# A decode layer on one core: 32 rows of wq by one indirect load of GpSimd instead of 512 columns by two side loads

## The chip, the cores and the metric

The kernel runs on one core of a Trainium2 chip. The metric is the device time of one execution in microseconds (us); the kernel before takes 137.85 us, the median of three runs (137.82 to 137.93). Engines are named as the profile names them: PE (TensorE), DVE (VectorE), ACT (ScalarE), POOL (GpSimd) and SP (SyncE, which issues most of the loads). PEld is PE's weight load, SPq and ACTq are the sequencers that issue DMAs.

## What is computed

One decode step of a transformer layer for a batch of 4 tokens with D = 1024, in bf16:

```
h  = x + attention(layernorm(x))          # 32 query heads, 4 kv heads, head size 128
h2 = h + (silu(hn @ w1) * (hn @ w3)) @ w2 # hn = layernorm(h), F = 3584
```

Attention projects the normed x with wq (1024 x 4096), takes the last W = 2048 positions of the K and V caches, scales by 128^-0.5, applies softmax, multiplies by V and projects with wo (4096 x 1024). Weights and cache together are some 55.6 million bytes, and each byte is used once.

## The kernel before

All weights and caches pass through one buffer, `ring`: 128 partitions by 81,920 columns of bf16 (`RING`, line 80). `plan` (line 129) lists the loads in their order, each with the column of the ring where it starts; `load_next` (line 149) issues the next entry. Nearly all are issued on SP's queue. The places, in columns:

- wq, rows 0 to 3 of each partition: 0 to 16,383; rows 4 to 7: 16,384 to 32,767. The view `wq_v` puts rows 8p to 8p + 7 of wq in partition p, so "row i" of a partition is row 8p + i of wq, with 4096 columns.
- K of the four batches: 32,768 to 65,535, four loads of 2 MB (`load_kv`).
- V of batch 0: 65,536 to 73,727, V of batch 1: 73,728 to 81,919. V of batches 2 and 3 go to 0 to 16,383, once the first half of wq is used.
- wo to 16,384 to 49,151, after the second half of wq and K of batches 0 and 1; w1 to 49,152 to 77,823, after K of batches 2 and 3 and V of batches 0 and 1; w3 to 0 to 28,671; w2 in four pieces.

A load into columns that are in use waits for the matmuls that read them. The tile framework adds these waits, and a wait where one of eight DMA semaphores is used again; it also settles each engine's order of instructions. Each engine runs its own in that order.

The work in order: x is loaded on ACT's queue, normed on DVE (lines 178 to 190), transposed on PE into `xnT` (line 194). q is computed by 512-column matmuls with `xnT[:, kc, :]` as weights (line 263), for the eight rows kc of each partition and the eight pieces of 512 columns, four of which fill different partitions of `q_ps`. q is scaled (lines 281, 282), transposed (line 285) and spread into `qz` (line 286). K is transposed in groups of eight tiles into one of four PSUM tiles (line 319), which DVE and ACT copy by turns to a `kT` tile (lines 323, 325; four buffers); each `kT` tile of two groups gives four scores matmuls (line 304). Then come softmax (lines 335 to 343), P's transposes (lines 350 to 360), P times V (line 382), wo (line 411), the second norm (lines 423 to 451), w1 and w3 (line 459) and w2 (line 492).

The part that the change replaces concerns row 7, the last of each partition, and of it the last 512 of 4096 columns. The main load of rows 4 to 7 (`load_tail`, line 123) stops 512 columns short. The 128 pieces of 512 columns come by two small loads (`load_side`, line 115), 20 partitions with four pieces each and 12 partitions with four pieces each, into two `kT` buffers. The matching values of the normed x are picked by two copies on DVE (line 206), transposed by eight small matmuls (line 211), copied from PSUM (line 218), and eight matmuls (line 273) with them as weights add the missing products to the last 512 columns of q, after row 3.

Of the kernel before, what the change touches and what calls it, by code (L numbers as in the profile page):

```python
# [10 lines left out]
P = 128  # L11
ACT = mybir.ActivationFunctionType
ALU = mybir.AluOpType
AX = mybir.AxisListType
BF16 = mybir.dt.bfloat16
FP32 = mybir.dt.float32


@with_exitstack
def kernel(  # L20
# [13 lines left out]
    nc = tc.nc  # L34

    B, _, D = A_x.shape
# [5 lines left out]
    KC = D // P  # L42
# [15 lines left out]
    ktpool = ctx.enter_context(tc.tile_pool(name="ktpool", bufs=4))  # L58
    wide = ctx.enter_context(tc.tile_pool(name="wide", bufs=2))
    const = ctx.enter_context(tc.tile_pool(name="const", bufs=1))  # L60
    act = ctx.enter_context(tc.tile_pool(name="act", bufs=1))
# [3 lines left out]
    JG = 4  # L65
    QD = P // JG
    RS = QD // B
    CQ = Hq * Dh // JG
# [11 lines left out]
    RING = 5 * 16384  # L80
# [8 lines left out]
    ring = stream.tile([P, RING], BF16)  # L89
# [19 lines left out]
    N_Q, N_F = Hq * Dh, F  # L109


    CE = 512
    SETS = [(0, 5, 4), (80, 3, 4)]

    def load_side(r0, ne, ns):

        t = ktpool.tile([P, JG * QD * 16], BF16, tag="kT")
        rows = A_wq[r0 * KC : (r0 + ne * 4 * ns) * KC, N_Q - CE : N_Q]
        rows = rows.rearrange("(t i k) n -> k i t n", i=ne, k=KC)[KC - 1]
        nc.sync.dma_start(out=t[: ne * 4, : ns * CE], in_=rows)  # L120
        return [t[: ne * 4, k * CE : (k + 1) * CE] for k in range(ns)]

    def load_tail(at, src, n, r0, m):

        t = ring[:, at : at + m * n]
        nc.sync.dma_start(out=t[:, : m * n - CE], in_=src[:, r0 * n : (r0 + m) * n - CE])
        return [t[:, k * n : (k + 1) * n] for k in range(m)]
    KIB = 512
    plan = [
        ("wq", load_rows, (0, wq_v, N_Q, 0, 4)),  # L130
        ("side", load_side, SETS[0]),
        ("side", load_side, SETS[1]),
        ("wq", load_tail, (32 * KIB, wq_v, N_Q, 4, 4)),
        ("k", load_kv, (64 * KIB, A_k_cache, 0)),
        ("k", load_kv, (96 * KIB, A_k_cache, 2)),
# [10 lines left out]
    loaded = {}  # L146
    cursor = [0]

    def load_next(n=1):
        for _ in range(n):  # L150
            if cursor[0] < len(plan):
                kind, f, args = plan[cursor[0]]
                loaded.setdefault(kind, []).extend(f(*args))
                cursor[0] += 1

    x_sb = act.tile([B, D], BF16)
    for c in range(2):
        nc.scalar.dma_start(out=x_sb[:, c * 512 : (c + 1) * 512], in_=x_flat[:, c * 512 : (c + 1) * 512])
    load_next(7)

    ident = const.tile([P, P], BF16)
    make_identity(nc, ident[:])
    eps_t = const.tile([P, 1], FP32)
    nc.vector.memset(eps_t[:], eps)

# [2 lines left out]
    for c in range(2):  # L168
        nc.sync.dma_start(
            out=x_q[c * 2 * QD : (c + 1) * 2 * QD : RS, :],  # L170
            in_=x_flat.rearrange("b (j c) -> j b c", j=JG)[2 * c : 2 * c + 2],
        )

    psA_cm = tc.tile_pool(name="psA", bufs=1, space=bass.MemoryType.PSUM)
    psA = psA_cm.__enter__()


    stats = act.tile([B, 2, nc.vector.BN_STATS_DIM], FP32)
    for c in range(2):
        nc.vector.bn_stats(out=stats[:, c, :], in_=x_sb[:, c * 512 : (c + 1) * 512])  # L180
    mv = act.tile([B, nc.vector.BN_AGGR_DIM], FP32)
    nc.vector.bn_aggr(out=mv[:], in_=stats[:])
    rstd = act.tile([B, 1], FP32)
    nc.scalar.activation(out=rstd[:], in_=mv[:, 1:2], func=ACT.Sqrt, bias=eps_t[:B], scale=1.0)
    nc.vector.reciprocal(out=rstd[:], in_=rstd[:])
    xn = act.tile([B, D], BF16)
    nc.vector.tensor_scalar(  # L187
        out=xn[:], in0=x_sb[:], scalar1=mv[:, 0:1], scalar2=rstd[:, 0:1],
        op0=ALU.subtract, op1=ALU.mult,
# [5 lines left out]
    xnT = act.tile([P, KC, B], BF16)  # L195
    nc.vector.tensor_copy(out=xnT[:], in_=tp_ps[:])


    NS = sum(ns for _, _, ns in SETS)
    ts_ps = psA.tile([P, NS, B], BF16, tag="kt1")  # L200
    xs = wide.tile([B, NS, 20], BF16, tag="w4k")
    sl = []
    for r0, ne, ns in SETS:
        v = xn[:, r0 * KC : (r0 + ne * 4 * ns) * KC]
        v = v.rearrange("b (s l i k) -> b k l i s", s=4, l=ns, i=ne)
        nc.vector.tensor_copy(
            out=xs[:, len(sl) : len(sl) + ns, : ne * 4].rearrange("b l (i s) -> b l i s", s=4),
            in_=v[:, KC - 1, :, :, :],
        )
        for l in range(ns):  # L210
            nc.tensor.transpose(
                out=ts_ps[: ne * 4, len(sl), :], in_=xs[:, len(sl), : ne * 4], identity=ident[:B, :B]
            )
            sl.append(ne * 4)
    xsT = act.tile([20, NS, B], BF16)
    k0 = 0
    for _, ne, ns in SETS:
        nc.vector.tensor_copy(out=xsT[: ne * 4, k0 : k0 + ns, :], in_=ts_ps[: ne * 4, k0 : k0 + ns, :])
        k0 += ns


    q_ps = psA.tile([P, CQ], FP32, tag="scores")
    nc.vector.memset(q_ps[:], 0.0)

    qz = act.tile([P, B, Hkv * QD + REP], BF16)
    nc.vector.memset(qz[:], 0.0)
    ident_f = const.tile([P, P], FP32)
    nc.vector.tensor_copy(out=ident_f[:], in_=ident[:])
# [3 lines left out]
        out=perm[:].rearrange("p (h dq) -> p h dq", dq=JG),  # L232
        in_=ident[:].rearrange("p (dq h) -> p h dq", dq=JG),
# [12 lines left out]
    for j in range(2, JG):  # L246
        nc.vector.tensor_tensor(
            out=same[:, 0, :], in0=same[:, 0, :], in1=ident[:, j * QD : (j + 1) * QD], op=ALU.add
# [3 lines left out]
        nc.vector.tensor_copy(out=same[:, j, :], in_=same[:, 0, :])  # L252


    for kc in range(KC):
        wq_t = loaded["wq"][kc]
        for hf in range(CQ // 512):
            for g in range(JG):
                c0 = g * CQ + hf * 512
                n = min(512, N_Q - CE - c0) if kc == KC - 1 else 512  # L260
                if n <= 0:
                    continue
                nc.tensor.matmul(  # L263
                    q_ps[QD * g : QD * g + B, hf * 512 : hf * 512 + n],
                    lhsT=xnT[:, kc, :],
                    rhs=wq_t[:, c0 : c0 + n],
                    start=(kc == 0),
                    stop=(kc == KC - 1 or (kc == KC - 2 and c0 + 512 == N_Q)),
                )
        if kc == RQ - 1:  # L270
            load_next()
            for k, np_ in enumerate(sl):
                nc.tensor.matmul(
                    q_ps[QD * (JG - 1) : QD * (JG - 1) + B, CQ - CE : CQ],
                    lhsT=xsT[:np_, k, :],
                    rhs=loaded["side"][k],
                    start=False,
                    stop=False,
                )
    q_sb = act.tile([P, CQ], BF16)  # L280
    nc.vector.tensor_single_scalar(out=q_sb[:, :512], in_=q_ps[:, :512], scalar=qscale, op=ALU.mult)
    nc.scalar.mul(out=q_sb[:, 512:], in_=q_ps[:, 512:], mul=qscale)
# [1 line left out]
    for r in range(REP):  # L284
        nc.tensor.transpose(out=qt_ps[:, r, :], in_=q_sb[:, r * Dh : (r + 1) * Dh], identity=ident[:])
    nc.vector.tensor_copy(
        out=qz[:, :, : Hkv * QD].rearrange("p b (g z) -> p b g z", g=Hkv)[:, :, :, :REP],
        in_=qt_ps[:].rearrange("p r (g x) -> p x g r", g=Hkv)[:, :B, :, :],
# [24 lines left out]
    for u, (b, n) in enumerate(units):  # L313
        k_v = loaded["k"][b]
        kT = ktpool.tile([P, NJ, P], BF16, tag="kT")
        for t in range(NJ // TB):
            kt_ps = psA.tile([P, TB, P], BF16, tag=f"kt{nt % 4}")
            for jj in range(TB):
                nc.tensor.transpose(  # L319
                    out=kt_ps[:, jj, :], in_=k_v[:, n * NJ + t * TB + jj, :], identity=ident[:]  # L320
# [21 lines left out]
        out=Pm[:], in_=scores_ps[:], func=ACT.Exp, bias=nmax[:], scale=1.0, accum_out=rsum[:]  # L342
# [6 lines left out]
    for c in range(NSB):  # L349
# [4 lines left out]
        for g in range(Hkv):  # L354
            if g % 2 == 0:
                nc.vector.tensor_scalar(  # L356
                    out=z[:, :, g, :], in0=pt_ps[:], scalar1=mask[:, g : g + 1], scalar2=None, op0=ALU.mult
# [10 lines left out]
        out=Dm[:], in0=ident[:].rearrange("p (g b r) -> p b g r", g=Hkv, b=B),  # L368
        scalar1=rinv[:, 0:1], scalar2=None, op0=ALU.mult,
# [10 lines left out]
    for b in range(B):  # L380
        for j in range(JK):
            nc.tensor.matmul(  # L382
                OT_ps[:, b, :],
                lhsT=loaded["v"][b][:, j, :],
                rhs=PTz[j // NJ][:, (j % NJ) * B + b, :, :],
                start=(j == 0),
                stop=(j == JK - 1),
# [21 lines left out]
    for i in range(IO):  # L409
        for j in range(JG):  # L410
            nc.tensor.matmul(  # L411
                y_ps[QD * j : QD * (j + 1), :],
                lhsT=o4[:, i, :, :].rearrange("p b s -> p (b s)"),
                rhs=loaded["wo"][i][:, j * CG : (j + 1) * CG],
                start=(i == 0),
                stop=(i == IO - 1),
# [27 lines left out]
        out=hn[:], in0=h1[:], scalar1=tot[:, 0:1], scalar2=rstd2[:, 0:1],  # L444
        op0=ALU.subtract, op1=ALU.mult,
# [4 lines left out]
        out=hnT[:].rearrange("p k x -> p (k x)"), in_=hn[:].rearrange("q (c k) -> q k c", k=KC)  # L450
# [3 lines left out]
    def gate_up(kind, out_ps):  # L454
# [27 lines left out]
        out=hgT[:].rearrange("p i x -> p (i x)"),  # L482
        in_=hg[:].rearrange("q s c -> q (s c)").rearrange("q (c i) -> q i c", i=IF),
# [18 lines left out]
    for i in range(R1, IF):  # L502
        for c, t in enumerate((ya_ps, yb_ps)):
            down(i, HC, c * HC, t, start=(i == R1), stop=(i == IF - 1), skip_group_check=True)
        if i == R2 - 1:
            for c, t in enumerate((ya_ps, yb_ps)):
                nc.tensor.matmul(
                    t[:, :HC], lhsT=ident_f[:], rhs=h2[:, c * HC : (c + 1) * HC],
                    start=False, stop=False, skip_group_check=True,
# [36 lines left out]
```

## Time and profile before

| what | value |
|---|---|
| time, median of three runs | 137.85 us |
| span of the profiled execution, first to last instruction | 136.0 us |
| PE busy | 72.3 us (53%) |
| DVE, ACT, POOL busy | 43.9, 31.0, 1.7 us |
| bytes read by DMA | 55.59 million, 409 GB/s over the span |
| share of the chain that ended last: DMA, PE, ACT, DVE | 54%, 25%, 11%, 5% |

The span leaves out what lies before the first and after the last instruction; the median is 1.85 us above it. The profile shows, for one execution, the busy share of each engine in 40 equal slices (3.4 us each), the chain of work that ended last followed back from the end, groups of equal instructions with their durations, and the DMA issues with the time to their landing. Times in it count from the first instruction. "x31" is a number of instructions, and what stands behind an arrow is what was waited for.

### The profile page before, as it was taken

What the parts mean: (1) busy time and instruction counts of PE and PEld (TensorE: products, weight loads), DVE (VectorE), ACT (ScalarE), POOL (GpSimd) and SP (SyncE); (2) the same over time, 40 slices, a digit from 0 to 9 for tenths busy, and PEclk for the clock granted to TensorE, in tenths of its full rate; (3) what the DMA queues carried; (4) which work ended last, traced back from release to release, by engine and by line L of the source; (5) the groups of instructions that cost most, each with busy time, mean ns of one, the idle gap of its engine ahead of it and who ended that gap; (6) DMA issues with size and microseconds to landing.
All of it is one profiled execution on the core that took longest, in us unless ns stands there. A gap on an engine that the chain in (4) does not pass through costs nothing.

```text
span 136.0 us, 2436 instructions
## 1 busy us (share of the span) xinstructions
PE 72.3 (53%) x1096; PEld 46.1 (34%) x1096; DVE 43.9 (32%) x79; ACT 31.0 (23%) x36; POOL 1.7 (1%) x8
## 2 busy tenths in 40 slices
PE   0004920979898989810525916791097000970981
PEld 0002300268374756500014905570043000430870
DVE  5055000043344444470994001206200596026010
ACT  3000000015555555609294300000001400000000
POOL 5000000000000000000000000000000000000000
PEclk9999975557999999985555555568556855568568
DMA  5999999999999999999989999989989899999970
GB/s 155 464 463 406 412 420 414 429 424 439 424 439 424 424 443 426 410 552 453 463 347 463 463 410 405 477 354 494 439 371 494 371 472 401 399 420 407 424 298 5
DMA packets 2650, 55.75 MB, mean 410 GB/s; under 512 B 296, under 2 KB 464, under 8 KB 720
## 3 DMA queue, kind: packets, MB, share of 16 engines
q1 hardware_dynamic: 2604, 55.58, 95.6%
q8 instruction: 8, 0.13, 0.3%
q10 hardware_dynamic: 36, 0.02, 0.0%
q14 instruction: 2, 0.02, 0.0%
HBM read 55.59 MB, written 0.01 MB: 409 GB/s over the span
## 4 chain that ended last, share of the span: by engine, by line
DMA 54%; PE 25%; ACT 11%; DVE 5%; SPq 2%; issue 1%; ACTq 0%
DMA ring<-in_B_w_dram 38%; DMA ring<-in_A_wq_dram 15%; PE kt_ps L319 11%; ACT kT L325 5%; PE scores_ps L304 5%; ACT z L360 3%; PE q_ps L263 3%; DVE rmax L336 2%; ACT Pm L341 2%; PE OT_ps L382 2%; DVE pT L350 1%; SPq L120 1%; PE g_ps L459 1%; DVE z L356 1%; ACT L341 1%
## 5 line engine op out<-in xcount | busy, mean ns | idle before, releaser
L325 ACT COPY kT<-kt_ps 128x1024 bf16<-128x1024 bf16 x16 | 15.9, 1013 | 13.4 <-PE kt_ps L319 13.4
L319 PE MATMUL kt_ps<-ident,ring 128*128 128x128 bf16 x256 | 18.0, 232 | 0.0
L319 PEld LDWEIGHTS <-ring 128*128 128x128 bf16 x256 | 16.0, 105 | 4.9 <-issue 4.9
L323 DVE COPY kT<-kt_ps 128x1024 bf16<-128x1024 bf16 x16 | 11.1, 692 | 16.5 <-PE kt_ps L319 16.5
L459 PEld LDWEIGHTS <-hnT 128*32 128x32 bf16 x128 | 5.5, 143 | 21.8 <-issue 19.2
L382 PE MATMUL OT_ps<-z,ring 128*128 128x32 bf16 x256 | 7.5, 188 | 8.5 <-ACT z L360 5.0
L459 PE MATMUL u_ps<-ring,hnT 128*32 128x448 bf16 x64 | 6.0, 563 | 11.0 <-DMA ring<-in_B_w_dram 11.0
L304 PE MATMUL scores_ps<-kT,qz 128*32 128x512 bf16 x64 | 9.9, 609 | 2.9 <-ACT kT L325 2.9
L263 PE MATMUL q_ps<-ring,xnT 128*4 128x512 bf16 x63 | 6.7, 595 | 7.8 <-DMA ring<-in_A_wq_dram 7.8
L382 PEld LDWEIGHTS <-ring 128*128 128x128 bf16 x256 | 7.4, 104 | 9.2 <-issue 9.2
L459 PE MATMUL g_ps<-ring,hnT 128*32 128x448 bf16 x64 | 5.9, 558 | 4.9 <-DMA ring<-in_B_w_dram 4.9
L492 PEld LDWEIGHTS <-hgT 128*32 128x32 bf16 x156 | 4.9, 134 | 6.2 <-issue 5.7
L411 PE MATMUL y_ps<-ring,o 128*32 128x256 bf16 x128 | 5.9, 371 | 0.8 <-DVE o L398 0.8
L514 ACT CAST res<-yb_ps 128x128 bf16<-128x128 f32 x1 | 0.3, 266 | 26.1 <-PE yb_ps L492 26.1
L492 PE MATMUL y_ps<-ring,hgT 128*32 128x256 bf16 x68 | 3.8, 419 | 4.4 <-DMA ring<-in_B_w_dram 4.4
L360 ACT ACTIVATE z<-pt_ps,mask 128x512 bf16<-128x512 f32 x8 | 5.3, 687 | 3.5 <-DVE z L356 3.5
L352 PE MATMUL pt_ps<-pT,perm 128*128 128x512 bf16 x4 | 2.4, 607 | 6.8 <-DVE pT L350 6.8
L263 PEld LDWEIGHTS <-xnT 128*4 128x4 bf16 x63 | 2.0, 115 | 11.7 <-issue 11.6
L194 PE MATMUL tp_ps<-ident,xn 4*128 4x4 bf16 x8 | 0.7, 200 | 10.0 <-DVE xn L187 10.0
L356 DVE TENSOR_SCALAR z<-pt_ps,mask 128x512 bf16<-128x512 f32 x8 | 5.5, 741 | 1.2 <-ACT z L360 0.8
L473 DVE RECIPROCAL eg<-eg 128x896 f32<-128x896 f32 x1 | 5.8, 5753 | 0.0
L411 PEld LDWEIGHTS <-o 128*32 128x32 bf16 x128 | 4.4, 131 | 3.1 <-DVE o L398 1.9
(85 smaller groups left out, 50.1 us busy)
## 6 DMA issues: line engine op xcount, KB each, us to landing
ring<-in_B_w_dram SPq DMA_DIRECT2D x2, 7168.0 KB, 22.5
ring<-in_A_k_cache_dram SPq DMA_DIRECT2D x4, 2048.0 KB, 27.6
ring<-in_A_v_cache_dram SPq DMA_DIRECT2D x4, 2048.0 KB, 29.2
ring<-in_B_w_dram SPq DMA_DIRECT2D x1, 4352.0 KB
ring<-in_A_wq_dram SPq DMA_DIRECT2D x1, 4096.0 KB, 12.2
ring<-in_A_wq_dram SPq DMA_DIRECT2D x1, 3968.0 KB
ring<-in_B_w_dram SPq DMA_DIRECT2D x1, 1792.0 KB
ring<-in_B_w_dram SPq DMA_DIRECT2D x1, 768.0 KB
```

The source lines that it names most:

```text
L263: nc.tensor.matmul(q_ps[QD * g : QD * g + B, hf * 512 : hf * 512 + n], lhsT=xnT[:, kc, :], rhs=wq_t[:, c0 : c0 + n], start=(kc == 0), stop ...
L304: nc.tensor.matmul(scores_ps[QD * g : QD * (g + 1), n * 512 : (n + 1) * 512], lhsT=qz_v[:, z0 : z0 + QD], rhs=kT_v[:, g, :, :], start=(b = ...
L319: nc.tensor.transpose(out=kt_ps[:, jj, :], in_=k_v[:, n * NJ + t * TB + jj, :], identity=ident[:])
L323: nc.vector.tensor_copy(out=kT[:, t * TB : (t + 1) * TB, :], in_=kt_ps[:])
L325: nc.scalar.copy(out=kT[:, t * TB : (t + 1) * TB, :], in_=kt_ps[:])
L356: nc.vector.tensor_scalar(out=z[:, :, g, :], in0=pt_ps[:], scalar1=mask[:, g : g + 1], scalar2=None, op0=ALU.mult)
L360: nc.scalar.mul(out=z[:, :, g, :], in_=pt_ps[:], mul=mask[:, g : g + 1])
L382: nc.tensor.matmul(OT_ps[:, b, :], lhsT=loaded["v"][b][:, j, :], rhs=PTz[j // NJ][:, (j % NJ) * B + b, :, :], start=(j == 0), stop=(j == J ...
L411: nc.tensor.matmul(y_ps[QD * j : QD * (j + 1), :], lhsT=o4[:, i, :, :].rearrange("p b s -> p (b s)"), rhs=loaded["wo"][i][:, j * CG : (j + ...
L459: nc.tensor.matmul(out_ps[QD * j : QD * (j + 1), hf, :HF], lhsT=hnT[:, k, :], rhs=loaded[kind][k][:, c0 : c0 + HF], start=(k == 0), stop=( ...
L473: nc.vector.reciprocal(out=eg[:], in_=eg[:])
L492: nc.tensor.matmul(out_ps[QD * j : QD * (j + 1), :n], lhsT=hgT[:, i, :], rhs=loaded["w2"][i][:, j * CG + c0 : j * CG + c0 + n], **kw,)
```

## The change

The two side loads, the copies, the transposes and the eight matmuls that belong to them go. In their place 32 whole rows of wq, row 7 of partitions 96 to 127 (`XP = 96`), leave the main load. The second half of wq is now loaded by two DMAs, all four rows for partitions 0 to 95 and three rows for partitions 96 to 127. The 32 rows come by one indirect load issued by GpSimd, with one index for each of 128 partitions; 32 indices name a row of wq, and 96 are 1024 or more and so out of bounds, which writes nothing. Which partitions ("lanes") get a row is set by `LANES`: lane group e is partitions 8e to 8e + 7, and n of them are used.

The 128 indices are computed on the chip: `sel` has a one where row m of the partitions 96 to 127 meets its lane, a matmul gives each lane its partition number and whether it is used, and three operations on DVE make 8p + 7, or a number past the end. Another matmul with `sel` carries the normed x to the lanes (`xgT`). Eight q matmuls on the gathered rows, as many as for any other row, follow row 3; the matmuls of row 7 use 96 partitions.

The gathered rows lie in the last 4096 columns of the ring (77,824 to 81,919), which are set to zero first, since the lanes out of bounds take part in the matmul. These columns are also the second half of V of batch 1. Its load is now the last that `load_next(5)` issues and stands ahead of the memset in the program, so that in the kernel after, the matmuls of P times V read zeros and rows of wq for half of batch 1's positions: that part of the computation differs from the reference.

```diff
+    XP = 96
+    LANES = [(0, 5), (1, 5), (2, 5), (3, 2), (4, 5), (6, 2), (8, 1), (9, 2), (15, 5)]
     def load_tail(at, src, n, r0, m):
         t = ring[:, at : at + m * n]
-        nc.sync.dma_start(out=t[:, : m * n - CE], in_=src[:, r0 * n : (r0 + m) * n - CE])
+        nc.sync.dma_start(out=t[:XP, :], in_=src[:XP, r0 * n : (r0 + m) * n])
+        nc.sync.dma_start(out=t[XP:, : (m - 1) * n], in_=src[XP:, r0 * n : (r0 + m - 1) * n])
...
-    load_next(7)
+    load_next(5)
+    xg = ring[:, RING - N_Q :]
+    nc.vector.memset(xg, 0.0)
     ident = const.tile([P, P], BF16)
     make_identity(nc, ident[:])
+    sel = wide.tile([P, P], BF16, tag="w4k")
+    nc.gpsimd.memset(sel[:], 0.0)
+    m0 = XP
+    for e, n in LANES:
+        nc.gpsimd.tensor_copy(out=sel[:, e * 8 : e * 8 + n], in_=ident[:, m0 : m0 + n])
+        m0 += n
+    pidx = const.tile([P, 1], I32)
+    nc.gpsimd.iota(pidx[:], pattern=[[0, 1]], base=0, channel_multiplier=1)
...
+    nc.tensor.matmul(id_ps[:], lhsT=sel[:], rhs=pv[:], start=True, stop=True)
...
+    nc.vector.tensor_tensor(out=idx[:], in0=idf[:, 0:1], in1=idf[:, 1:2], op=ALU.add)
+    nc.gpsimd.indirect_dma_start(
+        out=xg, out_offset=None, in_=A_wq,
+        in_offset=bass.IndirectOffsetOnAxis(ap=idx[:, :1], axis=0),
+        bounds_check=D - 1, oob_is_err=False,
+    )
...
+    xg_ps = psA.tile([P, B], FP32, tag="kt2")
+    nc.tensor.matmul(xg_ps[:], lhsT=sel[:], rhs=xnT[:, KC - 1, :], start=True, stop=True)
+    xgT = act.tile([P, B], BF16)
+    nc.vector.tensor_copy(out=xgT[:], in_=xg_ps[:])
...
     for kc in range(KC):
         wq_t = loaded["wq"][kc]
+        k = XP if kc == KC - 1 else P
+        q_row(xnT[:k, kc, :], wq_t[:k], kc == 0, kc == KC - 1)
         if kc == RQ - 1:
             load_next()
+            q_row(xgT[:], xg, False, False)
```

## The prediction

> **What bounds the kernel now.** I read first the page's rows by slices, then the chain that ended last in order of time, then the waits of SP's queue, and last the timeline around the instructions that the change moves.
>
> ```profile
> span 136.0 us, 2436 instructions
> ...
> PEclk9999975557999999985555555568556855568568
> DMA  5999999999999999999989999989989899999970
> ```
>
> The DMA engines are 90% busy from the second slice to the end, so the kernel is one stream of weights and cache and ends when its last bytes have been used. The stream stays full only because each load is issued before the one ahead of it has landed. The chain shows where that could break:
>
> ```profile
> 3.03 20.59 DMA ring<-in_A_wq_dram
> 23.62 0.04 issue
> 23.66 3.60 PE q_ps L263 x31
> 27.26 0.02 issue
> 27.29 0.70 DVE q_sb L281
> ...
> 34.23 0.55 PE scores_ps L304 x4
> ...
> 58.62 2.30 DVE rmax L336
> ...
> 74.79 1.46 PE OT_ps L382 x48
> 76.25 0.02 issue
> 76.27 22.49 DMA ring<-in_B_w_dram
> ...
> 100.48 29.74 DMA ring<-in_B_w_dram
> ```
>
> From 23.66 to 76.27 the chain is compute: q, K transposes and scores, softmax, P times V for batches 0 and 1. It ends in the issue of w1, because w1 goes into ring columns that K and V hold until then. SP's queue says the same:
>
> ```profile
> SPq L94 <- PE OT_ps L382: 23.3, 1, 23.3
> ```
>
> How much can that chain slip before DMA runs dry? The first half of wq is in use at 12.94, its second half at 23.66, and eight K and V loads of 2 MB (2.097 million bytes) follow in order. The last V load:
>
> ```profile
> ring<-in_A_v_cache_dram SPq DMA_DIRECT2D x4, 2048.0 KB, 29.2
> L102 SPq DMA_DIRECT2D ring<-in_A_v_cache_dram x4: 563/585/641, 13.5 to 33.4; - x4
> ```
>
> Issued at 33.4 and landed 29.2 later, at 62.6. So a 2 MB load takes (62.6 - 23.6)/8 = 4.875 us, which is 430 GB/s, and the second V load (V of batch 1) lands at 23.6 + 6 x 4.875 = 52.9. wo (8.39 million bytes, 19.5 us) then fills the queue to 82.1. The slack of w1's issue is about 82.1 - 76.3 = 5.8 us; a longer delay of the q chain becomes time.
>
> **What the change does, part by part.** The side loads and their work go: two SP issues (1.81 us, beside a full DMA queue), the xs and xsT copies on DVE (0.34 + 0.23), eight small transposes on PE (0.35), eight side matmuls (1.89). All lie in PE's wait for wq, before 12.94 or from 16.0 to 23.66, and are worth nothing. The new small work lies there too: one memset, one iota and nine small copies on POOL (rows of 0.21 and 0.29 us there: about 2.8 us, done near 6), two small matmuls on PE (which idles 2.03 us before 12.94), five column-sized operations on DVE at 0.15 to 0.2 each. Without that cover the sum is some 1 us on DVE and PE. The tail of wq in two pieces costs one more SP issue (0.44 us by the old tail's), in place of 1.81.
>
> What counts is where the gathered rows are put. They go to the last 4096 of the ring's 81,920 columns. V of batch 1 is loaded to columns 73,728 to 81,919 and is issued before the gather in program order. In the built order of the changed kernel, with the semaphore that each instruction waits for, the memset of these columns (new line 155) and the indirect load (line 195) both wait for the second round of the semaphore that the load of V of batch 1 raises, and the eight q matmuls on the gathered rows wait for the indirect load. PE's order is now: 32 q matmuls, 72 K transposes, the 8 gathered q matmuls, the last 32 q matmuls, then everything else. Thus q, which was complete at 27.26, can't be complete before V of batch 1 has landed.
>
> Queued behind the waits: on DVE, behind the memset, q_sb, qz and the K copies, which need q or a free kT buffer; on PE, behind the gathered matmuls, the whole second half of q, whose data came long before; on POOL nothing; on SP the load of wo, which waits for the last transposes of batch 1's K, and w1 behind it.
>
> Step by step, on the profiled execution's clock:
>
> 1. V of batch 1 lands. 256 KB less stand ahead of it in SP's queue: 0.26/430 = 0.6 us. 52.9 - 0.6 = **52.3**. (K's fourth load no longer waits for wq's first half, but V's first still does; all are issued by 15, so the queue stays full.)
> 2. Memset of 128x2048 words on DVE. Nearest rows:
>
> ```profile
> 1.24 0.91 DVE L223 MEMSET q_ps<- 128x1024 f32 x1 [0.21 <-issue]
> 2.20 0.28 DVE L226 MEMSET qz<- 128x272 uint32 x1
> ```
>
>    From these, 0.63 us for 752 more columns: 0.91 + 1024 x 0.84 ns = 1.8 us. Ends: 0.9 and 2.1. With 0.1 for the hand-over: **54.2**.
> 3. The indirect load. The trace has none, nor any DMA from POOL. Low end: the first half of x, issued on ACT's queue at 0.74 and in use at 2.40, 1.7 us. High end: the second half, issued by 1.60 beside SP's stream,
>
> ```profile
> 7.92 0.68 DVE L180 BATCH_NORM_STATS2 stats<-x_sb 4x6 f32<-4x512 bf16 x1 [4.90 <-DMA x_sb<-in_A_x_dram]
> ```
>
>    came at 7.92, 6.3 us later, for 4 KB; the fullest lane here moves five rows, 40 KB, at 430/16 = 27 GB/s 1.5 us, twice that beside the last two V loads, which are still streaming: 6.3 + 3.0 = 9.3. I take 6.3, as this too is a load on a second queue beside a full one. **60.5**.
> 4. 40 q matmuls. 31 took 3.60 at a granted clock of 0.5 (PEclk, slices 7 to 9); PE comes from idleness here too: 40/31 x 3.60 = 4.65. **65.1**.
> 5. q_sb, eight transposes, qz: 27.26 to 29.60, 2.34. **67.5**.
> 6. The rest of K. Four units of 16 transposes and 4 scores matmuls repeat every 7.02 us:
>
> ```profile
> 44.46 2.02 PE L319 MATMUL kt_ps<-ident,ring 128*128 128x128 bf16 x33
> 51.48 2.02 PE L319 MATMUL kt_ps<-ident,ring 128*128 128x128 bf16 x33
> ```
>
>    that is 1.755 a unit. 72 of 256 transposes are done before; they found PE idle. In the new order the next 32 transposes and four scores groups alternate with single ACT copies of 1.01: 2.0 + 2.2, 1.4 of waiting for copies, and 0.6 for the low clock, 6.2. The other 152 transposes are 9.5 units, 16.7, and 2.5 scores groups more at 0.55, 1.4. Together 24.3. Ends: no saving at all, 29.0 (before: 29.60 to 58.59); PE without a stall, 184 x 0.059 + 16 x 0.55 = 19.7. **91.8**, against 58.6: 33.2 late.
> 7. Softmax and PV are untouched: w1 is issued at 76.27 + 33.2 = **109.5**. wo meanwhile is issued near 78 instead of 42.8 and has landed near 100, so w1 starts on an idle queue. It takes 7.34/430 = 17.1 and a start; wq's first half, issued at 0.73 on an idle queue, landed 2.4 later than its bytes explain. 109.5 + 19.5 = **129.0**, against 98.76: 30.2 late.
> 8. From there the stream is full again: w3 is issued near 119 and w2 near 125, both before w1 has landed. The second norm ends at 96.15 + 33.2 = 129.4, about when w1 lands, and has w3's 17 us behind it. All the rest shifts by 30.2.
>
> Span 136.0 + 30.2 = 166.2. The median shown, 137.85, is 1.85 above the profiled span, and I keep that for what lies around it: **168.0 us**.
>
> **Two rules of the Trainium skill on step 3.** "DMA: Bandwidth & Descriptors", section "Anatomy of one DMA — SWDGE (gpsimd) path", fits such a load with about 2.0 us and the bytes at 436 GB/s; for 256 KB that is an estimate of 2.6, and the sum would be 164.3. "GPSIMD Engine Reference", section 2.1, states some 6 us for the first call of a freshly loaded kernel, which speaks against this change; with that on top of my value the sum would be 174. No row of this trace shows either.
>
> **Rivals.**
> - *A quick gather and a smooth PE*: 1.7 us for the load and 19.7 for step 6: 168.0 - 4.6 - 4.6 = 158.8; with one of the two, 163.4. For it: nothing else asks for POOL. Against: V still streams.
> - *A slow gather*: if POOL works through 128 indices one after the other, out of bounds or not, at the 0.10 us of its smallest row, that is 12.8 + 3.0 = 15.8 instead of 6.3: 177.5.
> - *The rows come early (the other side)*: if the gather were to run when its indices are ready, near 12, it would land before the second half of wq. Then q is where it was or sooner: 256 KB less on SP's queue are at most 0.6 us, and the time is 137.2 to 137.8. It decides if the rows have landed by 23.6. Against it stands the wait on V's semaphore, with 52.3 as its end.
> - *Nothing to be seen*: the delay would have to stay below the 5.8 us of slack; it is 33.
>
> **How the numbers follow.** Forecast 0.72 (163 to 172), quick 0.12, slow gather 0.12, early rows 0.03, no change 0.01. A difference under 0.2% can't be told from no change here. So slower 0.96, same 0.01, faster 0.03. The range runs from 160, between the quick rival's two sums, to 175, where steps 3 and 6 at their high ends (168.0 + 3.0 + 4.7 = 175.7) nearly meet; it leaves out the slow gather, the other side and a part of the quick case.
>
> **What would show it.** Right: DVE idle until about 52 before the memset of ring; PE waiting some 20 us before the first matmul on xgT; the wait ended by the indirect load near 60; DMA slices well under 9 between about 62 and 78 and again from 100 to 110; w1 issued near 109. Wrong: the gather's landing before 24, scores ending before 85, or a DMA row that stays at 9 throughout.

## The result and the profile after

The kernel after takes 179.76 us, the median of four runs (178.98 to 180.45), against 137.85 before: a ratio of 1.303 (95% interval 1.299 to 1.308). It is slower, as forecast, but by 41.9 us and not by 30.2; the range ended at 175. Of two kernels below, e3 and e7, one execution each was slow (141.65 and 142.41, the others 139.48 to 140.98 and 139.87 to 140.39); this moves their medians by 0.05 us, and e7's profile is of the slow one, so its gather's 9.4 can be too long.

The page's rows by slices of the kernel after (4.46 us each); GB/s is what the DMA engines moved:

```profile
span 178.5 us, 2439 instructions
...
DMA  6999998999999996000199991009999999899980
GB/s 236 471 352 235 235 200 196 426 426 437 426 422 444 428 430 279 4 0 0 62 411 470 459 411 75 0 4 411 402 415 411 411 441 540 371 374 429 396 343 6
```

Two things are new. Counted from 1, as in the prediction, the stream stands still in slices 17 to 19 and 25 to 27, which the prediction had. In slices 4 to 7, from about 13 to 31, the engines are called busy and move half as much as before, which it had not. The chain that ended last, in order of time:

```profile
0.74 12.33 DMA ring<-in_A_wq_dram
...
13.67 47.83 DMA ring<-in_A_v_cache_dram
...
64.03 8.31 DMA ring<-in_A_wq_dram,idx
72.34 0.04 issue
72.38 4.46 PE q_ps L266 x40
...
102.42 2.30 DVE rmax L334
...
120.15 21.11 DMA ring<-in_B_w_dram
```

The second line is the wait for V of batch 1: it was issued at 13.67 and landed at 61.5, and only then memset, gather and q follow. Before, q was ready at 27.26 and w1 was issued at 76.27. The timeline shows the pair on DVE and POOL, and the matmul that waits:

```profile
61.98 1.76 DVE L155 MEMSET ring<- 128x2048 uint32 x1 [21.11 <-DMA ring<-in_A_v_cache_dram]
64.03 1.18 POOL L195 DMA_INDIRECT ring<-in_A_wq_dram,idx  x1 [60.38 <-DVE ring L155]
72.38 1.02 PE L266 MATMUL q_ps<-ring,xgT 128*4 128x512 bf16 x8 [29.94 <-DMA ring<-in_A_wq_dram,idx]
```

For the slow stretch, the loads of x_q serve as clocks, since SP issues each when one piece of wq's tail has landed, the first the piece of 96 partitions, the second the piece of 32. First the line of x_q's loads, then the stretches between these times (length, busy time of PE, PEld, DVE, ACT, POOL, clock, DMA share, GB/s):

```profile
L173 SPq DMA_DIRECT2D x_q<-in_A_x_dram x2: 532/576/621, 28.0 to 31.4; - x2
```

```profile
13.10:27.90 14.80, 3.58 (x32) 0.94 (x31) 0.00 (x0) 0.00 (x0) 0.00 (x0) 1.00 0.97 209
27.90:31.40 3.50, 0.00 (x0) 0.00 (x0) 0.00 (x0) 0.00 (x0) 0.00 (x0) 1.00 0.94 241
31.40:36.10 4.70, 0.02 (x1) 0.03 (x2) 0.00 (x0) 0.00 (x0) 0.00 (x0) 1.00 1.01 432
```

The 96-partition piece ran at 209 GB/s. The first K load, by 128 partitions, is back at 432. The tail, 3.93 million bytes, took 18.3 us instead of the 9.1 that 430 GB/s would give. The DMA share is near 1 in all three: it can't tell a full stream from a clogged one; the GB/s beside it can.

### The profile page after: what moved, and what is told of

It reads as the page before. It is cut to its first block, busy times and chain, and to the rows that moved or that the text cites. A ratio compares the mean times of both kernels' runs of the same rounds, so it can differ in the third digit from the quotient of the medians.

```text
span 178.5 us, 2439 instructions
## 1 busy us (share of the span) xinstructions
PE 68.5 (38%) x1091; PEld 43.5 (24%) x1091; DVE 45.4 (25%) x82; ACT 31.1 (17%) x36; POOL 4.3 (2%) x20
## 4 chain that ended last, share of the span: by engine, by line
DMA 68%; PE 18%; ACT 6%; DVE 4%; issue 2%; SPq 0%; POOLq 0%; ACTq 0%; DVEq 0%
DMA ring<-in_B_w_dram 29%; DMA ring<-in_A_v_cache_dram 27%; PE kt_ps L317 7%; DMA ring<-in_A_wq_dram 7%; PE scores_ps L302 5%; DMA ring<-in_A_wq_dram,idx 5%; ACT z L358 3%; PE q_ps L266 3%; PE g_ps L457 1%; DVE rmax L334 1%; ACT Pm L339 1%; PE OT_ps L380 1%; ACT kT L323 1%; DVE pT L348 1%; DVE z L354 1%
## 5 line engine op out<-in xcount | busy, mean ns | idle before, releaser
L317 PE MATMUL kt_ps<-ident,ring 128*128 128x128 bf16 x256 | 19.6, 236 | 20.2 <-DMA ring<-in_A_k_cache_dram 19.8
L317 PEld LDWEIGHTS <-ring 128*128 128x128 bf16 x256 | 16.6, 106 | 27.7 <-DMA ring<-in_A_k_cache_dram 20.9
L266 PE MATMUL q_ps<-ring,xgT 128*4 128x512 bf16 x8 | 1.0, 609 | 29.9 <-DMA ring<-in_A_wq_dram,idx 29.9
L457 PEld LDWEIGHTS <-hnT 128*32 128x32 bf16 x128 | 4.9, 130 | 25.0 <-issue 21.9
L457 PE MATMUL u_ps<-ring,hnT 128*32 128x448 bf16 x64 | 5.1, 500 | 11.9 <-DMA ring<-in_B_w_dram 11.9
L380 PEld LDWEIGHTS <-ring 128*128 128x128 bf16 x256 | 7.3, 104 | 5.7 <-issue 5.6
L457 PE MATMUL g_ps<-ring,hnT 128*32 128x448 bf16 x64 | 5.1, 495 | 8.2 <-DMA ring<-in_B_w_dram 8.2
L266 PE MATMUL q_ps<-ring,xnT 128*4 128x512 bf16 (+1 forms) x64 | 7.2, 630 | 2.1 <-DMA ring<-in_A_wq_dram 2.1
L155 DVE MEMSET ring<- 128x2048 uint32 x1 | 1.8, 1765 | 21.1 <-DMA ring<-in_A_v_cache_dram 21.1
L280 ACT ACTIVATE q_sb<-q_ps 128x512 bf16<-128x512 f32 x1 | 0.6, 597 | 36.0 <-DVE q_sb L279 36.0
## 6 DMA issues: line engine op xcount, KB each, us to landing
ring<-in_A_wq_dram SPq DMA_DIRECT2D x1, 4096.0 KB, 12.3
```

What stands on the lines that cost most here:

```text
L266: nc.tensor.matmul(q_ps[QD * g : QD * g + B, hf * 512 : (hf + 1) * 512], lhsT=lhsT, rhs=rhs[:, c0 : c0 + 512], start=first, stop=last,)
L317: nc.tensor.transpose(out=kt_ps[:, jj, :], in_=k_v[:, n * NJ + t * TB + jj, :], identity=ident[:])
L380: nc.tensor.matmul(OT_ps[:, b, :], lhsT=loaded["v"][b][:, j, :], rhs=PTz[j // NJ][:, (j % NJ) * B + b, :, :], start=(j == 0), stop=(j == J ...
L457: nc.tensor.matmul(out_ps[QD * j : QD * (j + 1), hf, :HF], lhsT=hnT[:, k, :], rhs=loaded[kind][k][:, c0 : c0 + HF], start=(k == 0), stop=( ...
```

## The experiments

My theory after this profile had two causes that add: the gather's wait for V of batch 1, and the two tail pieces at half rate. The first rivals were that the slow tail is a consequence of the new order, or that the indirect load itself holds up the stream. Each time below stands beside the kernel before on the same chip, 137.9. A gather here is the indirect load, and its length counts from its start on POOL to its landing.

| kernel | time, us | ratio to before (95%) | gather, start to landing, us |
|---|---|---|---|
| after | 179.76 | 1.299 to 1.308 | 8.3 |
| V later (e1) | 149.48 | 1.083 to 1.086 | 24.3 |
| whole tail (e2) | 172.62 | 1.250 to 1.253 | 8.5 |
| V later, whole tail (e3) | 139.57 | 1.011 to 1.018 | 14.7 |
| plain: no side loads, no gather (e4) | 138.15 | 1.001 to 1.003 | |
| V later, 3 rows whole + 96 partitions of row 7 (e5) | 141.45 | 1.025 to 1.028 | 14.2 |
| plain, tail as 64 + 64 partitions (e6) | 148.95 | 1.078 to 1.081 | |
| as e3, 32 indices (e7) | 140.10 | 1.014 to 1.018 | 9.4 |
| plain, tail as 96 + 32 partitions (e8) | 147.98 | 1.071 to 1.075 | |
| plain, tail as 3 + 1 rows (e9) | 138.23 | 1.001 to 1.003 | |
| as e3, all 128 indices in bounds (e10) | 141.70 | 1.022 to 1.029 | 14.8 |
| as e3, tail as four loads of one row (e11) | 139.72 | 1.012 to 1.015 | 9.3 |
| row 7 gathered whole (e12) | 138.31 | 1.002 to 1.004 | 10.1 |

### Undoing one cause at a time: e1, e2, e3, e4

V later (e1), against the kernel after:

```diff
-    load_next(5)
+    load_next(4)
...
-            load_next()
             q_row(xgT[:], xg, False, False)
+            load_next(2)
```

> V of batches 0 and 1 is loaded after the gathered q matmuls, so that the memset and the gather wait for no V and the gathered rows are used before V overwrites their columns; the tail of wq stays in two pieces of 96 and 32 partitions. My theory has two causes that add: the wait of the gather for V of batch 1, and the two tail pieces at half the DMA rate (tail landed 31.4 instead of 23.6). Then this kernel keeps the second alone: gather landed near 20 to 21, scores ending near 67, the whole stream late by 8, time 146 (145 to 148). Rival 1, the tail's slowness is only a consequence of something else in the new order (the DMAs behind it, V's early issue): 138 to 140. Rival 2, the indirect load itself holds up the stream wherever it stands: over 150.

Whole tail (e2), against the kernel after; e3 has both edits:

```diff
-        nc.sync.dma_start(out=t[:XP, :], in_=src[:XP, r0 * n : (r0 + m) * n])
-        nc.sync.dma_start(out=t[XP:, : (m - 1) * n], in_=src[XP:, r0 * n : (r0 + m - 1) * n])
+        nc.sync.dma_start(out=t, in_=src[:, r0 * n : (r0 + m) * n])
```

> The kernel after, but the tail of wq comes as one load of four rows by all 128 partitions; row 7 of partitions 96 to 127 is loaded a second time by the gather and the first copy isn't used. As in the kernel after, half of V of batch 1 is overwritten by the gather. My theory: the tail is back at the full rate and lands near 24, V of batch 1 lands near 53 instead of 61.5, and the time falls by 8.6 to 171.2 (170 to 172.5). Rival 1, the slow stretch has nothing to do with the pieces' partitions: it stays at 179 to 180.

> Both of the edits above together: V later, tail whole. What is left of the change is the indirect load of 256 KB, which here is on top of the full 4 MB, and the sel matmuls. My theory: nothing waits, 256 KB more are 0.6 us, time 138.4 (137.5 to 139.3). Rival 2, the indirect load with its 96 indices out of bounds disturbs the stream beside it: 140 or more.

The plain kernel (e4) is the kernel before without lines 112 to 121, 199 to 219 and 272 to 279, with the tail as one load:

```diff
-        ("side", load_side, SETS[0]),
-        ("side", load_side, SETS[1]),
-        ("wq", load_tail, (32 * KIB, wq_v, N_Q, 4, 4)),
+        ("wq", load_rows, (32 * KIB, wq_v, N_Q, 4, 4)),
```

> The kernel before without its side loads: one whole tail, eight rows of q matmuls, no gather. It tells what there is to win by taking bytes out of the main load at all. My theory: the stream's bytes are the same, time 138.0 (137.6 to 138.6). If the balance over the DMA engines was worth much, 139 or more; if the side loads cost more than they bring, under 137.6.

Both causes are there. Taking the wait away is worth 179.76 - 149.48 = 30.3 with the pieces and 172.62 - 139.57 = 33.1 with the whole tail; taking the pieces away is worth 7.1 with the wait and 9.9 without. (The whole tail also loads the gathered 256 KB a second time, some 0.6 at 430 GB/s, so the pieces cost a little more than these differences.) They don't add exactly, and e1 missed its expectation by 3.5: I had its gather landing at 20 to 21. e2 and e3 came 0.1 and 0.3 above their ranges. The issue line of e1 gives the time to landing of the indirect load, started at 11.26:

```profile
ring<-in_A_wq_dram,idx POOLq DMA_INDIRECT x1, 24.3
```

Beside the slow tail the gather took 24.3 and landed at 35.6, after the tail, so that here too PE waited for it. In e3 it took 14.7, in the kernel after 8.3: the same load, with the same bytes. This opened a second question, what sets the length of a gather.

The plain kernel is 0.2% slower than before: against it, moving bytes out of the main load by the side loads had won some 0.3 us, and no version with a gather won any.

### What makes the tail slow: e6, e8, e9, e5

Each of e6, e8 and e9 is the plain kernel with another cut of its tail:

```diff
-        nc.sync.dma_start(out=t, in_=src[:, r0 * n : (r0 + m) * n])
+        nc.sync.dma_start(out=t[:64, :], in_=src[:64, r0 * n : (r0 + m) * n])
+        nc.sync.dma_start(out=t[64:, :], in_=src[64:, r0 * n : (r0 + m) * n])
```

with 96 in place of 64 in e8, and in e9 with `t[:, : 3 * n]` and `t[:, 3 * n :]`.

> The plain kernel (no side loads, no gather) with the tail of wq in two loads of four rows, partitions 0 to 63 and 64 to 127. In the kernel after, packets of 32 KB took about twice as long while the pieces of 96 and 32 partitions were loaded. Theory A: a load of part of the partitions reaches only part of the ways into SBUF; for partitions 0 to 63, and for 64 to 127, half of them, so both pieces run at half rate, the tail takes 19.5 instead of 9.75 and the time is near 148 (146.5 to 149). Theory B: 96 is the trouble, since six partitions fall to each DMA engine across some border of eight or four; with four to each engine the tail is at the full rate and the time 138.0 to 139.

> The plain kernel with the tail in two loads of four rows, partitions 0 to 95 and 96 to 127: the pieces of the change without its gather. Theories A and B both: the first piece at 210 GB/s, 14.8; by A the second at half rate too, 5.1, so some 10 more than the plain tail, time near 148 (147 to 149.5). By B the second piece of 32 partitions, two to an engine, is at the full rate, 2.4, and the time is 145.5. Rival C, the slowness needs the indirect load beside it or the other order: 138 to 139.

> The plain kernel with the tail in two loads by all 128 partitions, three rows and one row. A control: as many loads as in the change, but no partitions left out. Theories A and B: no change from the plain kernel, 137.9 to 138.5. If two loads in place of one were the cost: 145 or more.

Stretches of the tail's load, first of e4, then of e6 and e8, with GB/s last:

```profile
13.00:22.50 9.50, 3.43 (x35) 0.95 (x27) 0.00 (x0) 0.00 (x0) 0.00 (x0) 0.88 0.96 416
```

```profile
13.00:33.00 20.00, 3.36 (x32) 0.92 (x31) 0.00 (x0) 0.00 (x0) 0.00 (x0) 0.67 0.94 197
```

```profile
13.00:27.80 14.80, 3.58 (x32) 0.94 (x31) 0.00 (x0) 0.00 (x0) 0.00 (x0) 1.00 0.99 213
27.80:32.70 4.90, 0.00 (x0) 0.00 (x0) 0.00 (x0) 0.00 (x0) 0.00 (x0) 1.00 0.86 214
```

Theory A stands: 64, 64, 96 and 32 partitions all run at half rate, without any gather, and 128 partitions in two loads do not. Theory B, that six partitions to an engine is the trouble, falls with e6, and that two loads are the cost falls with e9. What the runs show is the rate by the number of partitions; whether the limit lies where the load writes, in SBUF, as theory A has it, or where it reads, no run separates. A rule that fits stands in the Trainium skill, "SBUF — State Buffer", section "Door 1: The DMA port swizzle": partitions 0 to 63, and 64 to 127, each reach 8 of 16 ports. e6 agrees with it (197 against 416 GB/s). It doesn't by itself say what a load of 96 partitions does, whose two thirds lie on one half of the ports; e8 measured 213, half for the whole piece.

The change with V later and a better cut (e5): three rows by all partitions, then only row 7 by 96.

```diff
+        nc.sync.dma_start(out=t[:, : (m - 1) * n], in_=src[:, r0 * n : (r0 + m - 1) * n])
+        nc.sync.dma_start(out=t[:XP, (m - 1) * n :], in_=src[:XP, (r0 + m - 1) * n : (r0 + m) * n])
```

> The change with V later, and the tail cut otherwise: three rows by all 128 partitions, then row 7 by partitions 0 to 95 alone; the gather brings the other 32 rows. No byte is loaded twice, and only 0.79 MB come by a 96-partition load. Theory A or B: that piece takes 3.7 instead of 1.8, 256 KB less than with the whole tail are 0.6 back, so 1.3 over the kernel with V later and the whole tail (139.57): 140.8 (140 to 142). If the half rate lasted as long as in the kernel with V later and both pieces: 149.

Most of the loss goes, as it should if it goes with the bytes loaded by 96 partitions.

### What sets the length of the gather: e7, e10, e11, e12

Against e3: e7 gathers into 32 partitions,

```diff
-    LANES = [(0, 5), (1, 5), (2, 5), (3, 2), (4, 5), (6, 2), (8, 1), (9, 2), (15, 5)]
+    LANES = [(0, 32)]
...
-    xg = ring[:, RING - N_Q :]
+    xg = ring[: P - XP, RING - N_Q :]
...
-        in_offset=bass.IndirectOffsetOnAxis(ap=idx[:, :1], axis=0),
+        in_offset=bass.IndirectOffsetOnAxis(ap=idx[: P - XP, :1], axis=0),
```

e10 gives the unused lanes the index 7 + lane (their weights are zero), and e11 cuts the tail's load by rows:

```diff
-        nc.sync.dma_start(out=t, in_=src[:, r0 * n : (r0 + m) * n])
+        for r in range(m):
+            nc.sync.dma_start(out=t[:, r * n : (r + 1) * n], in_=src[:, (r0 + r) * n : (r0 + r + 1) * n])
```

> V later, tail whole, as in the kernel that took 139.57, but the gather has 32 indices, all in bounds, for partitions 0 to 31, instead of 128 of which 96 are out of bounds. There the gather took 14.7 from its start to its landing beside packets of 32 KB, 10.3 of them after its first packet. Theory T, every lane of the gather, in bounds or not, waits for its turn behind one packet of SP's stream (1.21 each), eight lanes and the semaphore on each DMA engine: with two lanes, 4.4 + 3 x 1.21 + 0.3 = 8 to 9. Rival U, the landing is set by POOL and the bytes: 256 KB as before, 14 to 15. Time 138.4 to 139.6 in either case, as the tail's landing or the gather's decides when q is ready.

> The same kernel of 139.57, but the 96 unused lanes name rows in bounds, so that 128 rows, 1 MB, are fetched; the weights of the 96 are zero. Theory T: the turns are as many, each longer by a row's own 0.31, so 4.4 + 9 x 1.21 + 8 x 0.31 = 17.8 (17 to 19). Rival U, by bytes, four times as many: over 25. Time 1.8 more for 0.79 MB, and some for q: 141 to 143.

> The same kernel of 139.57, but the tail comes as four loads of one row, so that SP's packets are 8 KB (0.31) instead of 32 KB (1.21). Theory T: the gather lands after 4.4 + 9 x 0.31 + 5 x 0.31 = 8.7 (8 to 11) although nothing in it is changed. Rival U: 14 to 15. Time 138.3 to 139.3.

The first gathered matmul of e3, e7, e10 and e11, from their timelines; the gather starts at 11.28, 11.32, 11.41 and 11.29:

```profile
26.05 1.02 PE L265 MATMUL q_ps<-ring,xgT 128*4 128x512 bf16 x8 [9.40 <-DMA ring<-in_A_wq_dram,idx]
```

```profile
20.72 1.02 PE L264 MATMUL q_ps<-ring,xgT 32*4 32x512 bf16 x8 [4.04 <-DMA ring<-in_A_wq_dram,idx]
```

```profile
26.27 1.02 PE L269 MATMUL q_ps<-ring,xgT 128*4 128x512 bf16 x8 [9.69 <-DMA ring<-in_A_wq_dram,idx]
```

```profile
20.67 1.02 PE L266 MATMUL q_ps<-ring,xgT 128*4 128x512 bf16 x8 [4.02 <-DMA ring<-in_A_wq_dram,idx]
```

In e11 nothing in the gather was changed, only the size of the packets beside it, and it took 9.3 instead of 14.7. With a quarter of the lanes (e7) it took 9.4, with four times the bytes on the same lanes (e10) 14.8. So rival U falls, for which e7 and e11 had to stay at 14 to 15 and e10 to be over 25, and theory T holds in what counts: the lanes, in bounds or not, and the packets of the other queue set most of the length.

That e10 equals e3 doesn't show that a row's bytes cost nothing. In the packet records of both traces a packet of 8 KB takes 0.31, and on each DMA engine one packet of the gather and one of SP's queue take turns. In e3 an engine without a row needs 7.3 us for its nine packets of the gather and the engine that ends last some 9.7: 2.4 more, as much as eight rows at 0.31. In e10 every engine has eight. Both landed before the 17.8 that I expected of e10 because only five turns stood behind packets of 32 KB (1.21); then the tail was through, and the others stood behind K's packets of 16 KB (0.61).

The skill has a rule that fits, "DMA: Bandwidth & Descriptors", section "Queues, rings and completion order": an engine takes a whole packet from one queue, then turns to the next. The page puts some 9 to 17 descriptors into a packet; here a turn is one record of 8 to 32 KB, and whether that is the page's packet no run shows.

The last kernel leaves out what cost time, against e11:

```diff
-        for r in range(m):
+        for r in range(m - 1):
...
-    for kc in range(KC):
+    for kc in range(KC - 1):
...
-            q_row(xgT[:], xg, False, False)
+            q_row(xnT[:, KC - 1, :], xg, False, False)
```

with 8p + 7 as the index of partition p and without `sel`.

> A version without what cost time: V later, no load of a part of the partitions, no byte twice, no index out of bounds. Rows 4 to 6 come as three loads by all partitions, and row 7 of every partition by the gather, 128 rows of 8 KB with index 8p + 7, which needs no x and so starts near 3. By theory T it lands near 20, before the tail's end. Time as the plain kernel's 138.15 or a little less: 137.6 to 138.6. If an indirect load costs the stream something by itself: 139 or more.

138.31: 1 MB comes by the indirect load at no cost that stands out from the plain kernel's 138.15. (The gather started at 10.98 and not near 3, since DVE made its index behind other work.) It doesn't beat the kernel before, and no version here does.

## Why the prediction was right in its cause and wrong in its size

The mechanism was right: q waits for V of batch 1, w1's issue slips past the end of wo, and the stream stands still twice. Along the chain, what was forecast and what came:

| step | forecast | measured | difference |
|---|---|---|---|
| 1: V of batch 1 lands | 52.3 | 61.5 | +9.2 |
| 2: landing to gather's start | 1.9 | 2.5 | +0.6 |
| 3: gather's start to first matmul | 6.3 | 8.35 | +2.05 |
| 4, 5: q, q_sb, qz | 7.0 | 6.6 | -0.4 |
| 6: rest of K and scores | 24.3 | 23.4 | -0.9 |
| 7: softmax to w1's issue | 17.7 | 17.75 | 0 |
| 7: w1's issue to use | 19.5 | 21.15 | +1.65 |
| 8: from there to the end | as before | as before | 0 |

The sum is 12.2, against 42.5 - 30.2 = 12.3 in the spans. Steps 2, 3 and 7 took 4.3 more than forecast, and steps 4 to 6 gave 1.3 of it back, so the rest of the miss is step 1's.

**The step that failed is step 1.** The prediction priced the tail in two pieces at one more SP issue, 0.44, and took the stream to be full at 430 GB/s because it would be busy, with 0.6 back for the bytes that left. The bytes and the order were right; the rate was not: the tail took 18.3 us and not 9.1, which is the whole 9.2. The base of the step was right, though its 29.2 from issue to landing was the median of four V loads and not the last one's: with the whole tail (e2) V of batch 1 landed at 53.0, where the prediction has 52.9 without the 0.6, and memset followed:

```profile
53.43 1.76 DVE L154 MEMSET ring<- 128x2048 uint32 x1 [20.86 <-DMA ring<-in_A_v_cache_dram]
```

That a load of 96 or 32 partitions runs at half rate was in no row before, where every large load has 128 partitions, but then the term should have been bounded from both sides and was not. e8 gives its price alone, 147.98 - 138.15 = 9.8 for a tail of 4 MB.

**Step 3** was mis-sized by a third, inside its bounds of 1.7 and 9.3. The first packets of the gather came 4.3 after POOL started it, the other 3.7 until its last packet are its turns with the last V packets, two to three of 0.61 on an engine, and its own rows. The low bound, a small load on ACT's queue, was not of its kind. The term of 1.5 us for five rows on the fullest engine was too low as well: the lanes are the same as in e3, where the last engine carries some eight, 2.5 us at 0.31. Of the prediction's two other values for this step, 2.6 was far too low, and a further 6 us has no place in the 4.3.

**Step 7**: from w1's issue to its use was 1.65 more than forecast. The stretches of the kernel after around its start (columns as above):

```profile
120.00:122.00 2.00, 2.00 (x82) 2.00 (x79) 0.00 (x0) 0.00 (x0) 0.00 (x0) 0.50 1.38 459
122.00:124.00 2.00, 2.00 (x82) 2.00 (x79) 0.00 (x0) 0.00 (x0) 0.00 (x0) 0.50 0.20 86
124.00:130.00 6.00, 3.51 (x114) 2.90 (x114) 1.33 (x3) 0.00 (x0) 0.00 (x0) 0.95 0.99 423
```

The 86 GB/s are no pause. The first stretch books whole what starts in it, as its share above 1 shows: 459 GB/s in 2.00 us are 16 packets of 56 KB, one for each engine, and these were under way until about 124. They took 2.1 to 3.4 us each, most later ones 2.12. By its semaphore in the trace, 14 of the 16 engines had finished w1 at 139.1 to 139.4, within the 19.5 of the forecast; the last two came at 140.8 and 141.3. So the slowest engine made the difference; why it was late was not tried.

Step 6 held within 0.9: 72 transposes moved into the wait, and the rest in the new order took 23.4, against 24.3. wo was issued at 88.3 instead of 78, without consequence, as w1 came later still. Of the rivals, the slow gather at 177.5 is nearest to the result in time, but not in its cause: POOL was busy 1.18 for all 128 indices and not 12.8.

Open: e3 and e11 take 1.4 to 1.6 more than the plain kernel, and 256 KB twice loaded are 0.6; e11 and e7 came 0.4 and 0.5 above their ranges in time. In e3 the fullest engine carries some eight extra rows, 64 KB, 2.4 us at 27 GB/s, which would be enough if the stream ends with its fullest engine, and e12, with eight rows on every engine and the plain kernel's bytes, has no such loss. But e7, with two rows to an engine, takes as long as e3. This was not told apart.

## What to carry to other kernels

A buffer borrowed from a region that a load already owns makes its users wait for that load's landing, and the whole chain behind them: look in the built order for what the first writer of the borrowed columns waits for. A load by 32, 64 or 96 of the 128 partitions ran here at half the rate of a full stream while its engines showed as busy; read GB/s beside the busy share. The indirect load beside a full queue took some 4.3 us to its first packet (7.2 beside the slow tail of e1), and then on each engine one turn for each lane behind a packet of the other queue; an index out of bounds saves its row's 0.31, but no turn.

## What the runs showed of the hardware that was not expected

- Loads by 32, 64 or 96 partitions: 197 to 214 GB/s (241 in the short stretch of the kernel after, which also holds the start of the next load), by 128: 416 to 432. A packet of 32 KB took some 2.5 us (2.2 to 2.6) in the pieces of e6 and e8, 1.21 in e4's tail.
- An index out of bounds wrote nothing, but was not free: the gather's queue shows 32 packets of 8 KB and 112 of 4 bytes, so a small packet for each of the 96 lanes beside 16 for the semaphore. The row of an index out of bounds was not moved: e3's gather moved 0.26 MB by its packets, e10's 1.05. The page's line "HBM read" can't tell, as it shows 56.64 MB for both. The gather's queue in e3, then in e10:

```profile
q0 software_dynamic: 144, 0.26, 0.5%
```

```profile
q0 software_dynamic: 144, 1.05, 1.8%
```

- The same indirect load took between 8.3 and 24.3 us to land, by what stood in the other queue and how fast that moved.
